# K kept in two rings of key tiles, and filled work spread in groups of six pairs

## The chip, the cores and the metric

The kernel runs on one core of one Trainium2 chip. The metric is the device time of one execution in microseconds (us); lower is better. The core has five engines with queues of their own: TensorE (PE in the profile; its weight loads are PEld), VectorE (DVE), ScalarE (ACT), GpSimd (POOL) and SyncE (SP, which here only issues DMAs).

## The reference

One transformer block on 2048 tokens of width 512, in float32, with modulation vectors made from a condition `c`:

```python
sa, ca, ga, sb, cb, gb = split(silu(c) @ w_mod)        # six vectors of 512
h = layernorm(x) * (1 + ca) + sa
q, k, v = heads(h @ wqkv)                              # 32 heads of 16
p = softmax(q @ k.T / 4)                               # full, 2048 x 2048 for each head
x = x + ga * ((p @ v) @ wo)
h = layernorm(x) * (1 + cb) + sb
x = x + gb * ((silu(h @ w_gate) * (h @ w_up)) @ w_down)   # inner width 1792
```

## The kernel before

Matrix operands are held as a high and a low part, and each product is the sum of three terms (high by high, high by low, low by high). For attention the three terms are stacked in the contraction: a head's 16 rows become 48 (`KR`), plus 2 rows for the shift of the softmax. So a head uses half of TensorE's 128 rows, and two matmuls on different row halves run side by side.

**Units.** The queries are cut into 4 chunks of 512, the heads into 8 groups of 4. A unit `u` (of 32) is one chunk and one head group. A unit has 16 steps, one for each tile of 128 keys; a step has 4 pairs, one for each head. There are 2048 pairs in all. A pair (`pair_of`) is

- a score matmul (`score`, L506): keys by queries, into a score bank; ScalarE takes its exponential (L508) into a tile `pt`;
- on the other row half a max matmul (`max_one`, L479), 20 steps (80 pairs) ahead: queries by 512 keys, into a max bank; VectorE takes the largest of each row (L481).

When the 64 maxima of a unit are there, `max_rows` reduces them (L486), and `rows` transposes -max with matmuls against `ident` and `minus` (L491 to L493), copies it as two rows (`mr`) and writes them by DMA (L497) into the last 2 contraction rows of that unit's `qop`. Against rows of ones in `kop` they shift the scores, so no exponential overflows. `max_rows` puts five entries into the list `side`; each pair runs one of them.

**Value product.** `pv_step` (L521) multiplies the exponentials with V in halves of a step, 4 matmuls on 32 columns each; `pvs` issues several halves in a burst after each group of pairs. V has a column of ones, so the sums of the exponentials (the denominators) come out with the product.

**Unit end.** `close_unit` copies the result to `o`, sends its denominators by DMA into `dn` (`out_a`, L532), loads K and q of unit `u + 3`, and sets later work by step with `at(step, f)`: `out_b` takes the reciprocal on VectorE (L536) and stores it, `out_r` loads it spread over 128 partitions (`rb`), `out_c` multiplies on POOL (L548) and stores the attention rows in DRAM. After the last unit of a chunk the rows are read back (`load_o`) and split (`split_o`).

**K.** Three whole buffers `kop[u % 3]` of 2048 keys; a unit's load (`load_k`, L404) is two DMAs of 768 KB, one issued by SP, one by POOL.

**Fills.** The rest of a chunk (output projection, norm, gate and up, down) fills TensorE's time under the pairs of later units. A job of `accumulate` yields one fill at a time, two matmuls on the two row halves (L718). Two schedules call `pair_of`:

- `plain(steps)`: windows of 3 pairs and then 1 or 2 halves of the value product; 4 max banks, 3 score banks;
- `filled(places, work)`: after pair `r` come `places[r]` fills, and after the group a burst of up to 6 halves; 3 max banks, 2 score banks (4 and 5), the other two hold the job's sums. A gate and up job has 24 fills in two groups `TWO` of 8 pairs, a down job 12 fills in two groups `ONE` of 4 pairs:

```python
TWO = (0, 3, 2, 2, 2, 2, 1, 0)
ONE = (0, 3, 3, 0)
```

In order: projections; a lead of 20 steps with maxima alone; then for chunk `ci` a plain lead to step `STARTS[ci]`, 4 groups of the output projection, 12 plain steps (norm, transposes), for the last of them `REST` more, then the jobs. A plain window (`WIN` steps) stands before a chunk's last down jobs. `posts` (run by `hook` after a group) holds VectorE's and POOL's part of a job. The last 7 jobs (`KEEP`) and the whole of chunk 3 come after the pairs, with full-height matmuls (L727).

`wo` (the output weights, in two `wgu` buffers), `wgu` and `wd` are split once during the first chunk and kept in DRAM (`wo_dr`, `gu_dr`, `wd_dr`).

Of the kernel before, what the change touches and what calls it, by code (L numbers as in the profile page):

```python
# [19 lines left out]
P = 128  # L20
# [26 lines left out]
REST = 24  # L47
NORM = 9
STARTS = (147, 275, 403)
TWO = (0, 3, 2, 2, 2, 2, 1, 0)  # L50
ONE = (0, 3, 3, 0)
ALONE = {TWO: ((0, 4, 0, 4, 0, 4, 0, 0), (4, 5, 0, 1, 5, 0, 4, 1)), ONE: ((0, 6, 0, 0), (4, 5, 4, 0))}

# [48 lines left out]
def block_kernel(ctx, tc, x, wqkv, wo, w_gate, w_up, w_down, c, w_mod, out):  # L102
# [21 lines left out]
    ident = const.tile([P, P], F32, name="ident")  # L124
    minus = const.tile([P, P], F32, name="minus")
    eps_t = const.tile([P, 1], F32, name="eps_t")
# [88 lines left out]
    kop = [vp.tile([P, 2, S], F32R, name="kop0"), None, None]  # L215
# [47 lines left out]
    nc.gpsimd.tensor_scalar_mul(minus, ident, -1.0)  # L263
# [137 lines left out]
    def load_parts(dst, src, g, c0, c1, second=nc.sync):  # L401
        heads = src[g * 64:(g + 1) * 64, :, c0:c1].rearrange("(s b d) r c -> b (d r) s c", s=2, b=2)
# [3 lines left out]
    def load_k0(ci):  # L406
        load_parts(kop[0][:, :, ci * CW:(ci + 1) * CW], kd, 0, ci * CW, (ci + 1) * CW)
# [3 lines left out]
    for b in range(2):  # L411
        nc.sync.dma_start(kop[0][64 * b + KR:64 * b + KR + 2].bitcast(F32).rearrange("p s (a c) -> p (s a) c", c=CW),
                          ones[:, None, :].to_broadcast([2, 2 * NC, CW]))
    kq = [(w, m) for m in range(NK) for w in (1, 0)]
    for ci in range(NC - 1):
# [12 lines left out]
        for i, _ in enumerate(sm.jobs(jobs)):  # L428
            if ci == 0 and i == 5:
                half_prep(1, ev)  # L430
                take(weights_, 2)
                sm.add("w", 5, weights_)
            if ci == 0 and i == 24:
                sm.add("p", 5, prep(pa, xt[1], hT[1], 0, 1))
            if i == 40:
                load_k0(ci)
            if i == 44 and ci + 2 < NC:
                load_x(ci + 2)
# [11 lines left out]
    kop[1] = pb.tile([P, 2, S], F32R, name="kop1", bufs=1)  # L450
    pf = None
    qop, mx, pts, pv, o_, due, res = {}, {}, {}, {}, {}, {}, {}
    posts = []
    n = 16 * NU
    last = NC - 1

    def ones_rows(k):
        for b in range(2):
            rows = slice(64 * b + KR, 64 * b + KR + 2)
            nc.sync.dma_start(kop[k][rows].bitcast(F32), kop[0][rows].bitcast(F32))  # L460

    def load_k(u):
        load_parts(kop[u % 3], kd, u % NG, 0, S, nc.gpsimd if u > 2 else nc.sync)

    def load_q(u):
        ci, g = divmod(u, NG)
        qop[u] = pb.tile([P, 2, CW], F32R, name="qop", tag="qop", bufs=3)
        load_parts(qop[u], qd, g, ci * CW, (ci + 1) * CW, nc.gpsimd if u > 2 else nc.sync)

    def max_one(r):  # L470

        u, t = divmod(r // 4, 16)
        b, e = 1 - r % 4 // 2, r % 2
        s, qt, kc = t // 8, t // 2 % 4, t % 2 * 2 + e
# [4 lines left out]
        nc.tensor.matmul(pm, qop[u][rows, s, qt * P:(qt + 1) * P], kop[u % 3][rows, s, kc * CW:(kc + 1) * CW],  # L479
# [3 lines left out]
    def max_rows(u):  # L483

        m = pb.tile([P, 16], F32, name="m", tag="m")
        nc.vector.tensor_reduce(m, mx.pop(u).rearrange("p b s t f -> p (b s t) f"), op=ALU.max, axis=AX.X)  # L486
        nm = pb.tile([P, 16], F32R, name="nm", tag="nm")

        def rows():
            pr = bank("pr")[0:16, 0:2 * P]  # L490
            nc.tensor.matmul(pr[:, 0:P], nm.bitcast(F32), ident, start=True, stop=True)  # L491
            nc.tensor.matmul(pr[:, P:2 * P], m, minus, start=True, stop=False)
            nc.tensor.matmul(pr[:, P:2 * P], nm.bitcast(F32), minus, start=False, stop=True)  # L493
            mr = pb.tile([16, 2, P], F32R, name="mr", tag="mr", bufs=1)
            nc.scalar.copy(mr, pr.rearrange("p (r q) -> p r q", r=2))
            for r in range(2):
                nc.sync.dma_start(qop[u][KR + r:KR + r + 65:64].bitcast(F32), mr[:, r, :].bitcast(F32))  # L497
        side.extend([lambda: None, lambda: None, lambda: nc.scalar.mul(nm, m, -1.0), lambda: None, rows])

    def score(i, h):  # L500
# [5 lines left out]
        nc.tensor.matmul(sp, kop[u % 3][rows, h // 2, kt * P:(kt + 1) * P], qop[u][rows, h // 2, :],  # L506
# [120 lines left out]
    class Chunk:  # L627
# [15 lines left out]
        def load_wo(self, places=None):  # L643
            self.wo = places or [as_wo(tile_gu()) for _ in range(NK // 2)]
            for k, w in enumerate(self.wo):
                (nc.sync if self.ci == 0 else nc.gpsimd).dma_start(w.bitcast(F32), wo_dr[k])

        def load_gu(self, f):
            if f < NF and f not in self.loaded:
                self.loaded.add(f)  # L650
                self.w[f] = self.places[f % len(self.places)] if self.places else tile_gu()
                nc.sync.dma_start(self.w[f].bitcast(F32), gu_dr[f])
# [99 lines left out]
    def out_pair(ch, t0, outs, halves):  # L752
        return accumulate(outs, lambda e, a, k: ch.oT[a][:, k, (t0 + e) * P:(t0 + e + 1) * P],
                          lambda b, k: ch.wo[k // 2][:, b, k % 2, :], NK,
                          lambda: posts.append(lambda: add_o(ch, t0, outs, True)), halves)

    def out_terms(ch, t, pt, ks):
        for k in ks:
            for a, b in ((0, 0), (0, 1), (1, 0)):
                nc.tensor.matmul(pt, ch.oT[a][:, k, t * P:(t + 1) * P], ch.wo[k // 2][:, b, k % 2, :],  # L760
                                 start=(k == 0 and a == b == 0), stop=(k == NK - 1 and a == 1))

    def gate_up(ch, f, outs, halves):
# [20 lines left out]
        return accumulate(outs, lambda e, a, k: w[:, 2 * e + a, k, :], lambda b, k: ch.hT[b][:, k, :], NK, after,  # L784
# [25 lines left out]
    def begin(ci):  # L810
        x2 = pf.tile([P, 4, D], F32, name="x2", tag="x2", bufs=1)
        act = [pf.tile([P, NK, CW], F32R, name=f"act{a}", tag=f"act{a}", bufs=1) for a in range(2)]
        hT = [pf.tile([P, NK, CW], F32R, name=f"act{a}", tag=f"act{a}", bufs=1) for a in range(2)]
        chunks[ci] = ch = Chunk(ci, x2, act, hT)
# [12 lines left out]

    late = sm.jobs([proj_T(last, w, m) for w, m in kq[:1] + kq[2:]] + [proj_T(last - 1, w, m) for w, m in kq[6:]] +
                   [proj_T(last, *kq[1])] + [proj_v(4 * ci + t) for ci in (last - 1, last) for t in range(4)])
    ones_rows(1)  # L830
    load_q(0)
    take(late, 22)
    load_k0(last)
    take(late, 26)

    def close_unit(u, i):
# [11 lines left out]
        if u % NG == NG - 1:  # L848
            if u // NG:
                at(i + 1, lambda: begin(u // NG))  # L850
                at(i + 1, lambda: chunks[u // NG].load_wo())
            at(i + 7, lambda: chunks[u // NG].load_o(nc.gpsimd))
            at(i + 9, lambda: chunks[u // NG].split_o())

    at(3, lambda: begin(0))
# [4 lines left out]
    def after(i):  # L860
# [6 lines left out]
        if i == -2:  # L867
# [4 lines left out]
            kop[2] = pf.tile([P, 2, S], F32R, name="kop2")  # L872
            ones_rows(2)
            load_k(2)
# [4 lines left out]
    for i in range(-LEAD, -1):  # L879
        if i == -LEAD + 3:  # L880
            load_k(1)
# [5 lines left out]
        while side:  # L887
            side.pop(0)()

# [15 lines left out]
    def pvs(most, by_halves):  # L905
# [4 lines left out]
        while most and halves and 4 * halves[0][0] + 8 <= done:  # L910
# [16 lines left out]
    def plain(steps, tails=()):  # L927
# [4 lines left out]
        for w in range(4 * steps // WIN):  # L932
            for _ in range(WIN):
                pair_of()
            if w >= 4 * steps // WIN - len(tails):
                tails[w - 4 * steps // WIN](four())
# [3 lines left out]
    def filled(places, work):  # L940
# [14 lines left out]
    def two_of(u):  # L955
        return [kop[u % 3][:, e, :].rearrange("p (k c) -> p k c", k=NK) for e in range(2)]

    def begin_last():
# [100 lines left out]
```

## Time and profile before

| | us |
|---|---|
| median of 3 runs | 1921.11 |
| the runs | 1927.79, 1919.36, 1921.11 |
| span of the profiled execution, first to last instruction | 1926.2 |
| TensorE busy in it | 1876.4 (97%) |
| VectorE busy | 1541.1 (80%) |
| ScalarE busy | 1250.8 (65%) |
| POOL busy | 418.6 (22%) |

The profile gives the span of its own execution; what that execution took as a whole is not told beside it. A busy share on TensorE is no measure of its rate, since matmuls overlap: the two of a pair run side by side, and so do the two of a fill. The views used below are the page itself; stages (busy time of each engine between two times, with the granted TensorE clock, the share of the DMA engines and GB/s at the end of each row); instructions in order of time (start, duration, engine, line, operation, shapes, and in brackets the idle time before it and what ended it); and waits (who waited for whom: total, times, longest).

### The profile page before, as it was taken

The page shows a single profiled execution, that of the slowest core. Times are in us where ns is not written, and L with a number is a line of the kernel's source. Part 1 is how long each engine was busy: PE and PEld are TensorE (multiplying, and loading weights), DVE is VectorE, ACT ScalarE, POOL GpSimd, SP SyncE. Part 2 cuts the span into 40 slices and gives each one's busy share as a digit, 9 for nine tenths or more (in the row PEclk, how much of TensorE's full clock was granted, in tenths as well). Part 3 has the DMA queues.
Part 4 walks back from the last instruction along what each step waited for, and adds up shares of the span by engine and source line. Part 5 has one row for each costly group of instructions (what it writes and reads, how often), then busy time and mean ns, then how long its engine had stood idle before and what let it go on. Part 6 is the DMA issues. An engine that isn't in the chain of part 4 may idle for free.

```text
span 1926.2 us, 40835 instructions
## 1 busy us (share of the span) xinstructions
PE 1876.4 (97%) x16996; PEld 1149.1 (60%) x16996; DVE 1541.1 (80%) x2558; ACT 1250.8 (65%) x2330; POOL 418.6 (22%) x504
## 2 busy tenths in 40 slices
PE   7999999999999999999899999999899999999999
PEld 5766444444455666666455666666455466667787
DVE  5458998999989888888789888888799988841643
ACT  4222887788877766667677766776677876674211
POOL 3000344555322211111123111111133011021200
PEclk9999999999999999999899999999899999999999
DMA  8764766667753534553544544453543354253642
GB/s 299 265 219 121 187 161 161 190 180 185 192 90 74 141 99 113 148 133 84 130 81 90 121 114 131 116 141 76 135 81 76 54 141 119 73 177 122 237 194 109
DMA packets 78340, 267.60 MB, mean 139 GB/s; under 512 B 17364, under 2 KB 22484, under 8 KB 57476
## 3 DMA queue, kind: packets, MB, share of 16 engines
q1 hardware_dynamic: 58188, 173.81, 31.7%
q0 software_dynamic: 19280, 90.39, 19.5%
q8 instruction: 133, 2.18, 0.5%
q10 hardware_dynamic: 688, 0.80, 0.1%
q14 instruction: 51, 0.42, 0.1%
HBM read 201.85 MB, written 62.13 MB: 137 GB/s over the span
## 4 chain that ended last, share of the span: by engine, by line
PE 89%; DMA 5%; DVE 3%; ACT 2%; SPq 0%; issue 0%; ACTq 0%; DVEq 0%
PE bank L521 25%; PE bank L506 20%; PE bank L718 18%; PE bank L479 9%; PE bank L727 7%; PE bank L209 6%; DMA dn<-o 4%; DVE mx L481 1%; PE bank L760 1%; PE bank L491 1%; DVE stt L743 1%; PE bank L162 0%; PE bank L703 0%; DMA wm_ab<-in_w_mod 0%; PE bank L493 0%
## 5 line engine op out<-in xcount | busy, mean ns | idle before, releaser
L481 DVE TENSOR_REDUCE mx<-bank 128x1 f32<-128x512 f32 x2048 | 1285.6, 683 | 146.9 <-PE bank L479 97.7
L479 PE MATMUL bank<-kop,qop 48*128 48x512 f32 x2048 | 766.2, 439 | 26.4 <-DVE mx L481 25.0
L506 PE MATMUL bank<-qop,kop 50*128 50x512 f32 x2048 | 757.4, 433 | 3.8 <-DMA qop<-mr 0.9
L506 PEld LDWEIGHTS bank<-qop,kop 50*128 50x128 f32 x2048 | 349.0, 187 | 315.6 <-issue 54.5
L479 PEld LDWEIGHTS bank<-kop,qop 48*128 48x128 f32 x2048 | 347.3, 187 | 59.2 <-DVE mx L481 42.4
L718 PE MATMUL bank<-act,wgu 64*128 64x512 f32 x1872 | 295.4, 393 | 0.0
L718 PEld LDWEIGHTS bank<-act,wgu 64*128 64x128 f32 x1872 | 184.3, 187 | 32.6 <-issue 0.2
L548 POOL TENSOR_TENSOR on<-o,rb 128x512 f32<-128x512 f32 x31 | 39.8, 1283 | 527.4 <-DMA rb<-d_dr 379.4
L718 PE MATMUL bank<-wd,mid 64*128 64x512 f32 x912 | 130.5, 392 | 0.0
L779 POOL CAST mid<-m 128x512 fp32r<-128x512 f32 x40 | 24.5, 612 | 345.4 <-PE bank L479 164.8
L209 PE MATMUL bank<-hT,wqs 128*128 128x512 f32 x384 | 95.8, 400 | 2.3 <-ACT hT L328 1.0
L718 PEld LDWEIGHTS bank<-wd,mid 64*128 64x128 f32 x912 | 88.7, 186 | 15.3 <-issue 0.7
L209 PEld LDWEIGHTS bank<-hT,wqs 128*128 128x128 f32 x384 | 70.4, 188 | 24.3 <-issue 6.1
L775 DVE SCALAR_TENSOR_TENSOR q<-th,bank 128x512 f32<-128x512 f32 x56 | 38.1, 681 | 56.8 <-ACT th L771 56.8
L771 ACT ACTIVATE th<-bank 128x512 f32<-128x512 f32 x56 | 33.3, 594 | 58.5 <-PE bank L727 58.4
L791 DVE TENSOR_TENSOR x<-bank,x 128x512 f32<-128x512 f32 x84 | 53.9, 685 | 19.6 <-PE bank L718 19.6
L369 DVE TENSOR_TENSOR prt<-bank,prt 128x512 fp32r<-128x512 f32 x32 | 22.0, 689 | 45.5 <-ACT prt L367 45.5
L367 ACT CAST prt<-bank 128x512 fp32r<-128x512 f32 x32 | 18.8, 586 | 58.6 <-PE bank L209 46.8
L777 DVE TENSOR_TENSOR m<-bank,q 128x512 f32<-128x512 f32 x56 | 38.7, 692 | 21.1 <-PE bank L727 19.1
L727 PE MATMUL bank<-wd,mid 128*128 128x512 f32 x216 | 52.3, 395 | 0.5 <-DVE mid L780 0.3
L780 POOL TENSOR_TENSOR mid<-m,mid 128x512 fp32r<-128x512 f32 x40 | 51.5, 1288 | 3.3
L718 PE MATMUL bank<-wgu,act 64*128 64x512 f32 x288 | 47.9, 395 | 0.1
(6282 smaller groups left out, 5196.9 us busy)
## 6 DMA issues: line engine op xcount, KB each, us to landing
wgu<-gu_dr SPq DMA_DIRECT2D x48, 1024.0 KB
wd<-wd_dr SPq DMA_DIRECT2D x28, 1024.0 KB
kop<-kd SPq DMA_DIRECT2D x33, 768.0 KB
kop<-kd POOLq DMA_DIRECT2D x29, 768.0 KB, 8.4
gu_dr<-wgu POOLq DMA_DIRECT2D x14, 1024.0 KB, 4.9
kd<-prt SPq DMA_DIRECT2D x16, 512.0 KB
qd<-prt SPq DMA_DIRECT2D x16, 512.0 KB
kop<-gu_dr SPq DMA_DIRECT2D x8, 1024.0 KB
```

The source lines that it names most:

```text
L209: nc.tensor.matmul(pt, lhs(a, k), rhs(b, k), start=(n == 0), stop=(n == 3 * nk - 1))
L479: nc.tensor.matmul(pm, qop[u][rows, s, qt * P:(qt + 1) * P], kop[u % 3][rows, s, kc * CW:(kc + 1) * CW], start=True, stop=True)
L481: nc.vector.tensor_reduce(mx[u][:, b, s, qt, kc:kc + 1], pm, op=ALU.max, axis=AX.X)
L506: nc.tensor.matmul(sp, kop[u % 3][rows, h // 2, kt * P:(kt + 1) * P], qop[u][rows, h // 2, :], start=True, stop=True)
L521: nc.tensor.matmul(pv[u][32 * h:32 * h + 32, cols], v_flat[:, e0:e0 + 32], p_[h][:, cols], start=(kt == 0 and half == 0), stop=(kt == 15), ...
L548: mul.tensor_mul(on, o, rb)
L718: nc.tensor.matmul(outs[e], lhs(e, a, k)[rows], rhs(b, k)[rows], start=(ph == 0 and j == 0), stop=(ph == 1 and j == z))
L727: nc.tensor.matmul(outs[e], lhs(e, a, k), rhs(b, k), start=(j == 0), stop=(j == z))
L775: nc.vector.scalar_tensor_tensor(q, th, 1.0, outs[0], op0=ALU.add, op1=ALU.mult)
L777: nc.vector.tensor_mul(m32, outs[1], q)
L780: (nc.gpsimd if slow else nc.vector).tensor_sub(mid[:, 1, :], m32, mid[:, 0, :].bitcast(F32))
L791: nc.vector.tensor_add(ch.x2[:, t, :], outs[e], ch.x2[:, t, :])
```

## The change

- K lives in two rings of four tiles of 512 keys, `kop[u % 2][c]`. Each tile is loaded for unit `u + 2` when unit `u`'s scores have passed it (`at(16 * u + 4 * c + 3, ...)`), by two DMAs of 192 KB, both on SP, as are q's. The maxima of a unit go through the key tiles in order.
- The memory of the third K buffer holds a second pair of activation tiles, so the attention rows of a chunk are read back and split two units at a time.
- Part of the jobs is spread thinner: groups `SIX` of 6 pairs and 6 fills. Gate and up jobs up to a limit (`THICK`, 8, 8 and 5 for the three chunks) take four of these in place of two `TWO`, down jobs two in place of two `ONE` (now called `FOUR`). The plain leads of chunks 1 and 2 come to length 0, the windows before the last down jobs go, `REST` is halved, `STARTS` are 3 steps earlier. After a group the burst is 3 halves where it ends in the middle of a step.
- The rows of -max come from two products instead of three, four pairs after the copy that they need, and at the end of a group, ahead of the burst.
- At a unit's end the reciprocal comes 5 steps after closing instead of 3, the spread load 6 instead of 4, the product 8 instead of 5.
- The output weights of the next chunk are loaded before a chunk's last down jobs. For the last chunk they go into the K ring as its tiles come free, and two gate and up tiles are loaded right after the pairs.
- `minus` is made on VectorE.

```diff
-REST = 24
-STARTS = (147, 275, 403)
+STARTS = (144, 272, 400)
+REST = 12
+THICK = (8, 8, 5)
 TWO = (0, 3, 2, 2, 2, 2, 1, 0)
-ONE = (0, 3, 3, 0)
+SIX = (0, 2, 2, 1, 1, 0)
+FOUR = (0, 3, 3, 0)
+LATE = (0, 0, 0, 3, 3, 0)
...
-    nc.gpsimd.tensor_scalar_mul(minus, ident, -1.0)
+    nc.vector.tensor_scalar_mul(minus, ident, -1.0)
...
+    def load_k(u, ci):
+        load_parts(kop[u % 2][ci], kd, u % NG, ci)
...
+    kop[1] = [pb.tile([P, 2, CW], F32R, name=f"kop1{c}", bufs=1) for c in range(NC)]
+    nms = [pb.tile([P, 2, 16], F32R, name=f"nm{e}", bufs=1) for e in range(2)]
...
     def max_one(r):
-        b, e = 1 - r % 4 // 2, r % 2
-        s, qt, kc = t // 8, t // 2 % 4, t % 2 * 2 + e
+        b, s = 1 - r % 4 // 2, r % 2
+        kc, qt = divmod(t, 4)
...
     def max_rows(u):
-        m = pb.tile([P, 16], F32, name="m", tag="m")
-        nc.vector.tensor_reduce(m, mx.pop(u).rearrange("p b s t f -> p (b s t) f"), op=ALU.max, axis=AX.X)
+        m = pb.tile([P, 2, 16], F32, name="m", tag="m")
+        for_rows = mx.pop(u).rearrange("p b s t f -> p (b s t) f")[:, None].to_broadcast([P, 2, 16, NC])
+        nc.vector.tensor_reduce(m, for_rows, op=ALU.max, axis=AX.X)
+        nm = nms[u % 2]
         def rows():
-            nc.tensor.matmul(pr[:, 0:P], nm.bitcast(F32), ident, start=True, stop=True)
-            nc.tensor.matmul(pr[:, P:2 * P], m, minus, start=True, stop=False)
-            nc.tensor.matmul(pr[:, P:2 * P], nm.bitcast(F32), minus, start=False, stop=True)
+            nc.tensor.matmul(pr, m.rearrange("p r h -> p (r h)"), minus, start=True, stop=False)
+            nc.tensor.matmul(pr, nm.rearrange("p r h -> p (r h)").bitcast(F32), ident, start=False, stop=True)
...
-        side.extend([lambda: None, lambda: None, lambda: nc.scalar.mul(nm, m, -1.0), lambda: None, rows])
+        wait = [lambda: None] * 3
+        side.extend(wait + [lambda: nc.scalar.copy(nm[:, 1, :], m[:, 0, :])] + wait + [lambda: tails.append(rows)])
...
+        def load_wo_part(self, k):
+            nc.gpsimd.dma_start(kop[0][k].bitcast(F32), wo_dr[k // 2][:, :, k % 2, :])
+            self.wo = lambda b, k: kop[0][k][:, b, :]
...
     def begin(ci):
+        oT, hT = [[pf.tile([P, NK, CW], F32R, name=f"act{ci % 2}{a}", tag=f"act{ci % 2}{a}", bufs=1) for a in range(2)]
+                  for _ in range(2)]
...
+    for c, t in enumerate(kop[1]):
+        for b in range(2):
+            own = slice(64 * b + KR, 64 * b + KR + 2)
+            nc.sync.dma_start(t[own].bitcast(F32), kop[0][c][own].bitcast(F32))
     load_q(0)
...
         if u + 3 < NU:
-            load_k(u + 3)
             load_q(u + 3)
-        at(i + 3, lambda: res.__setitem__(u, out_b(u, nc.sync, *res[u])))
-        at(i + 4, lambda: res.__setitem__(u, out_r(u, nc.sync, *res[u])))
-        at(i + 5, lambda: out_c(u, nc.gpsimd, nc.gpsimd, *res.pop(u)))
+        at(i + 5, lambda: res.__setitem__(u, out_b(u, nc.sync, *res[u])))
+        at(i + 6, lambda: res.__setitem__(u, out_r(u, nc.sync, *res[u])))
+        at(i + 8, lambda: out_c(u, nc.gpsimd, nc.gpsimd, *res.pop(u)))
+        if u % 2 and u < NU - 2:
+            at(i + 10, lambda: chunks[u // NG].load_o(nc.gpsimd, (u % NG // 2,)))
+            at(i + 12, lambda: chunks[u // NG].split_o((u % NG // 2,)))
+    for u in range(NU - 2):
+        for c in range(NC):
+            at(16 * u + 4 * c + 3, lambda u=u, c=c: load_k(u + 2, c))
...
     def filled(places, work):
         for r in range(len(places)):
             pair_of()
             take(work, places[r])
-            if r % 4 == 3:
-                end_steps()
+            end_steps()
         hook()
-        pvs(6, False)
+        flush()
+        pvs(3 if done % 4 else 6, False)
+
+    def window(ch, job, args):
+        thick = (args[0] if job is gate_up else 2 * args[0]) >= THICK[ch.ci]
+        if job is down:
+            if args == (NF // FG - 1, 0):
+                return (FOUR, FOUR) if thick else (LATE, SIX)
+            return (FOUR if thick else SIX,) * 2
+        return (TWO,) * 2 if thick else (SIX,) * 4
...
             if args == (NF // FG - 1, 0):
-                plain(WIN)
+                chunks[ci + 1].load_wo()
+            places = window(ch, job, args)
             work = job(ch, *args, outs, True)
-            for _ in range(2):
-                filled(TWO if job is gate_up else ONE, work)
+            for group in places:
+                filled(group, work)
+        if ci < last - 1:
+            rows_of(chunks[ci + 1])
...
+    ch.places = [[kop[r][2 * k + e] for e in range(2)] for r in (1, 0) for k in range(2)]
+    for f in range(2):
+        ch.load_gu(f)
```

More of the change, by code (lines that the diff above doesn't have):

```diff
@@ L214, in block_kernel @@
     vp = ctx.enter_context(tc.tile_pool(name="vp", bufs=1))
-    kop = [vp.tile([P, 2, S], F32R, name="kop0"), None, None]
+    kop = [[vp.tile([P, 2, CW], F32R, name=f"kop0{c}") for c in range(NC)], None]
     VW = NT * H * (DH + 1)
@@ L478, in max_one @@
         pm = four("pm")
-        nc.tensor.matmul(pm, qop[u][rows, s, qt * P:(qt + 1) * P], kop[u % 3][rows, s, kc * CW:(kc + 1) * CW],
+        nc.tensor.matmul(pm, qop[u][rows, s, qt * P:(qt + 1) * P], kop[u % 2][kc][rows, s, :],
                          start=True, stop=True)
@@ L505, in score @@
         sp = bank("st_")
-        nc.tensor.matmul(sp, kop[u % 3][rows, h // 2, kt * P:(kt + 1) * P], qop[u][rows, h // 2, :],
+        nc.tensor.matmul(sp, kop[u % 2][kt // 4][rows, h // 2, kt % 4 * P:(kt % 4 + 1) * P], qop[u][rows, h // 2, :],
                          start=True, stop=True)
@@ L810, in begin, with rows_of @@
     def begin(ci):
[L811 to L814, printed above, removed]
+        oT, hT = [[pf.tile([P, NK, CW], F32R, name=f"act{ci % 2}{a}", tag=f"act{ci % 2}{a}", bufs=1) for a in range(2)]
+                  for _ in range(2)]
+        chunks[ci] = Chunk(ci, None, oT, hT)
+    def rows_of(ch):
+        ch.x2 = pf.tile([P, 4, D], F32, name="x2", tag="x2", bufs=1)
         ch.load_x2(nc.gpsimd)
@@ L880, in block_kernel @@
         if i == -LEAD + 3:
-            load_k(1)
+            for c in range(NC):
+                load_k(1, c)
             load_q(1)
@@ L909, in pvs @@
             most, owed = most + owed, 0
-        while most and halves and 4 * halves[0][0] + 8 <= done:
+        while most and halves and 4 * halves[0][0] + (6 if done % 4 == 2 and not by_halves else 8) <= done:
             i, half = halves.pop(0)
@@ L925, in end_steps, with plain @@
             ended += 1
-    def plain(steps, tails=()):
+    def plain(steps, ends=()):
         nonlocal four, bank
@@ L934, in plain @@
                 pair_of()
-            if w >= 4 * steps // WIN - len(tails):
-                tails[w - 4 * steps // WIN](four())
+            if w >= 4 * steps // WIN - len(ends):
+                ends[w - 4 * steps // WIN](four())
+            flush()
             pvs((HALVES[(w - 2) % 4] if done > 8 else 0) + (w == 4 * steps // WIN - 1), True)
@@ L1023, in block_kernel @@
     take(rest, 48)
-    ch.places = [tile_gu() for _ in range(2)]
-    for u in (NU - 3, NU - 2):
-        ch.places += [kop[u % 3][:, k, :].rearrange("p (a k c) -> p a k c", a=4, k=NK) for k in range(2)]
-    ch.ahead = 4
-    for f in range(ch.ahead):
+    ch.places += [tile_gu() for _ in range(2)]
+    for f in range(2, ch.ahead):
         ch.load_gu(f)
```

98 lines of the change are left out of this document (44 added, 54 removed).

## The prediction

> **What bounds the kernel now.** I read the page's head first, then the stages cut at group boundaries, then the order of time inside one group, and last the waits of the stages that lose.
>
> ```profile
> span 1926.2 us, 40835 instructions
> PE 1876.4 (97%) x16996; PEld 1149.1 (60%) x16996; DVE 1541.1 (80%) x2558; ACT 1250.8 (65%) x2330; POOL 418.6 (22%) x504
> ```
> ```profile
> core 0: us, PE busy (x) PEld busy (x) DVE busy (x) ACT busy (x) POOL busy (x), PEclk, DMA share, GB/s
> 188.00:566.00 378.00, 370.00 (x3568) 170.95 (x3568) 357.60 (x606) 313.20 (x616) 171.85 (x176) 0.96 0.67 170
> 628.00:908.00 280.00, 280.00 (x2912) 185.09 (x2912) 240.83 (x382) 194.91 (x350) 42.17 (x49) 1.00 0.48 121
> 931.00:995.00 64.00, 55.05 (x510) 24.74 (x508) 51.26 (x87) 45.02 (x88) 16.58 (x23) 0.87 0.58 130
> 1360.00:1425.00 65.00, 56.75 (x510) 25.59 (x509) 51.31 (x87) 44.99 (x88) 16.54 (x23) 0.87 0.57 128
> 1487.00:1546.00 59.00, 58.58 (x590) 27.41 (x590) 58.12 (x99) 51.16 (x102) 6.79 (x8) 1.00 0.32 66
> 1762.00:1926.00 164.00, 159.79 (x720) 128.49 (x712) 69.31 (x117) 27.03 (x45) 10.77 (x14) 1.00 0.46 177
> ```
>
> A pair is one score and one max matmul. 1487 to 1546 is plain work of 96 pairs: 0.615 us a pair, and VectorE is busy for 58.1 of 59 us, so plain work sits on VectorE with TensorE just under it. 628 to 908 is filled work of chunk 0: VectorE has 39 us to spare and TensorE none. The three leads (588, 84 and 84 pairs) are plain too, but take 378, 64 and 65 us where 0.615 gives 361.6, 51.7 and 51.7: 16.4, 12.3 and 13.3 us are lost there.
>
> Inside one filled group:
>
> ```profile
> 709.53 0.42 PE L506 MATMUL bank<-qop,kop 50*128 50x512 f32 x1
> ...
> 711.75 0.50 PE L506 MATMUL bank<-qop,kop 50*128 50x512 f32 x1
> ...
> 712.09 0.40 PE L506 MATMUL bank<-qop,kop 50*128 50x512 f32 x1
> ...
> 713.02 0.41 PE L506 MATMUL bank<-qop,kop 50*128 50x512 f32 x1
> ...
> 713.96 0.40 PE L506 MATMUL bank<-qop,kop 50*128 50x512 f32 x1
> ...
> 715.30 0.49 PE L506 MATMUL bank<-qop,kop 50*128 50x512 f32 x1
> ```
>
> 711.75 to 715.30 is a group of 4 pairs and 6 fills (places 0, 3, 3, 0): the first two pairs are 0.34 apart, and three fills with the next pair take 0.93, so a place for a pair or a fill is 0.233 us. The last pair with two halves of the value product takes 1.34; 709.53 to 711.75 is the same with four halves, 2.22. A half is thus 0.44 us, and each burst of them costs 0.46 beside.
>
> A score bank is given back late:
>
> ```profile
> 708.37 0.39 PE L506 MATMUL bank<-qop,kop 50*128 50x512 f32 x1
> 708.80 0.60 ACT L508 ACTIVATE pt__7769<-bank 128x512 f32<-128x512 f32 x1
> 709.45 0.18 PEld L506 LDWEIGHTS bank<-qop,kop 50*128 50x128 f32 x1 [0.19 <-ACT pt__7769 L508]
> ```
> ```profile
> 712.29 0.60 ACT L508 ACTIVATE pt__7814<-bank 128x512 f32<-128x512 f32 x1 [1.22 <-PE bank L479]
> ```
> ```profile
> 712.32 1.89 DVE L481 TENSOR_REDUCE mx<-bank 128x1 f32<-128x512 f32 x3 [0.18 <-PE bank L479]
> ```
>
> With two score banks, the pair of 709.53 waited for the exponential of 708.37: 0.43 to its start, 0.60 for it, 0.13 to the next matmul, 1.16 in all; just after a burst the first part is 0.54 (711.75 to 712.29), 1.27 in all. Five places are 1.165, so the old groups just fit. Three maxima take 1.89, 0.63 each.
>
> **The change part by part.**
>
> *Groups.* Counted from the code, the filled work now takes 128 groups of 6 pairs and 6 fills. They replace 42 groups of 8, 44 groups of 4, and 252 plain pairs: the leads of chunks 1 and 2, 12 pairs of the first lead, 24 before the last down jobs, 48 of the rest.
> What goes: a group of 4 is 3.55 above, and I take 3.6 with unit ends; the 28 groups of 8 and 24 of 4 in 628 to 908 then give (280 − 86.4) / 28 = 6.91. So 42 × 6.91 + 44 × 3.6 = 448.6; the plain pairs are 64 + 65 + 84 × 0.615 = 180.7. Together 629.3 us.
> What comes: places 0, 2, 2, 1, 1, 0 with banks 4 and 5. Pair 1 at 0.34; pair 2 would be at 0.34 + 0.70 = 1.04, but its bank comes at 1.27; pair 3 at 1.97; pair 4 at 2.44 (its bank at 2.43); pair 5 would be at 2.90, its bank comes at 1.97 + 1.16 = 3.13; then 0.46 + 3 × 0.44 = 1.78. Sum 4.91, and 4.95 with the shares of -max rows and unit ends; 128 × 4.95 = 633.6.
> Net +4.3 us: four places instead of five between two users of a bank cost 0.46 a group, and eat what 39 bursts fewer would bring. Bounds: 4.50 if the bank waits do not bind (58 us less), and 5.3 if all six exponentials queue at 0.60 ahead of the burst (6 × 0.60 + 1.78; 45 us more). I take 4.95, nearest to the rows. VectorE needs 6 × 0.63 + 0.7 for the additions, 4.5, so it stays hidden by 0.45.
>
> *Later unit end and ring loads.* The losses of the leads are waits for the denominators:
>
> ```profile
> DVE dn L536 <- DMA dn<-o: 9.0, 5, 2.8
> ```
> ```profile
> DVE dn L536 <- DMA dn<-o: 9.5, 1, 9.5
> ...
> PE bank L479 <- DVE mx L481: 8.6, 1, 8.6
> ```
> ```profile
> 962.00:972.00 10.00, 10.00 (x69) 4.28 (x65) 6.85 (x12) 5.09 (x10) 4.16 (x6) 0.58 0.20 59
> ```
> ```profile
> 322.00:332.00 10.00, 8.97 (x57) 3.97 (x59) 7.46 (x13) 4.09 (x8) 0.00 (x0) 0.66 0.48 80
> ```
>
> The first row is of the first lead, the two next of chunk 1's. The reciprocal stands on VectorE ahead of the maxima, so TensorE stops for want of max banks, and then runs at a granted 0.58 to 0.66 for 10 us. Now the reciprocal comes two steps (8 × 0.615 = 4.9 us) later, more than the longest wait of the first lead (2.8), and the 1.5 MB of K no longer go out behind the denominators but in quarters. I count the 16.4 us of the first lead as gone; the two long ones are already in the 629.3, and their cause (x, output weights, K and q at once) is spread out. Bounds: −16.4 and 0.
> The Trainium skill ("TensorE: Matmul & The Clock Gate", Part 1) says that the clock is halved only after an idle window of about 3.4 us. By that, waits up to 2.8 us cost only themselves, 9.0 us, and the forecast below would be 1912. The row of 322 to 332 disagrees: 0.66 after a stop well under that.
> What the later end moves on POOL (scaling at +8, the read-back of attention rows at +10) lies on an engine that is 22% busy. Out jobs start 14 steps after their last unit closes.
> K's loads leave POOL's queue for SP's: eight issues a unit in place of two, each queued behind mr and the denominators. They are asked for nine steps (36 × 0.615 = 22 us) before they are read, against
>
> ```profile
> kop<-kd POOLq DMA_DIRECT2D x29, 768.0 KB, 8.4
> ...
> wgu<-wo_dr POOLq DMA_DIRECT2D x4, 1024.0 KB, 21.1
> ...
> kop<-wo_dr POOLq DMA_DIRECT2D x2, 1024.0 KB, 9.0
> ```
> 8.4 us for four times the bytes: nothing. Bounds 0 and the price of the slower rival below.
>
> *Rows of -max.*
>
> ```profile
> 704.05 0.49 PE L506 MATMUL bank<-qop,kop 50*128 50x512 f32 x1
> ...
> 704.49 0.39 PE L491 MATMUL bank<-ident,nm 128*16 128x128 f32 x2
> ...
> 705.25 0.50 PE L506 MATMUL bank<-qop,kop 50*128 50x512 f32 x1
> ```
> Two pairs are 1.20 apart where 0.34 is usual: 0.86 a unit for six instructions. Four remain, put ahead of a burst, and the copy they wait for is four pairs old: I take 0.5, so 0.36 × 19 units outside the new groups, −7 us (bounds −16 and 0). They are issued at least 8 pairs (4.9 us) before the scores that need them. VectorE's reduction reads twice the elements:
> ```profile
> L486 DVE TENSOR_REDUCE m<-mx 128x16 f32<-128x64 f32 x32 | 6.9, 216 | 0.9
> ```
> at most another 0.22 us a unit, under the slack of the groups; 0.
>
> *Start and end.* The ones rows of the second K take eight issues on SP instead of two ahead of the first q:
>
> ```profile
> 119.33 1.43 SPq L460 DMA_DIRECT2D kop<-kop  x2
> ```
> ```profile
> 131.95 0.59 PE L479 MATMUL bank<-kop,qop 48*128 48x512 f32 x2 [1.15 <-DMA kop<-kd]
> ```
> Six more at 0.72 are 4.3 us; the wait of 1.15 for the last part of K goes, since maxima now run by key tile. I take +2 (0 to +4). The minus matrix moves from POOL to an idle VectorE: 0. At the end TensorE is busy for 159.8 of 164 us, so earlier loads and the new places are worth 0 (−4 to +1).
>
> Sum: +4.3 − 16.4 − 7 + 2 = −17.1 us, off a span of 1926.2. What lies around the span is not shown; it is 5.1 us above the median of the runs, 1921.1, from which I take the same 17 us: 1904.
>
> **The rivals.**
> *Bank waits do not bind.* For it: ScalarE is at 65%. Against it: the 0.19 at 709.45. A group then takes 4.50, and 58 us more go: 1846.
> *Only the waits count, not the clock* (the skill's rule above): 1912.
> *The unit-end wait stays.* If the denominators land more than 5 steps after they are asked for, VectorE stops as now. For it: all of K, q, weights and rows are now on SP's queue. Against it: less is in flight at that moment. Half of the 42 us lost in the leads returns: 1925, no change.
> *Output weights late, the side of slower.* Their load now starts when the last gate job of a chunk ends, behind a cast and a subtraction on POOL:
>
> ```profile
> L779 POOL CAST mid<-m 128x512 fp32r<-128x512 f32 x40 | 24.5, 612 | 345.4 <-PE bank L479 164.8
> ...
> L780 POOL TENSOR_TENSOR mid<-m,mid 128x512 fp32r<-128x512 f32 x40 | 51.5, 1288 | 3.3
> ```
> With the issues that is 3 us, and four groups of 4 (14.4 us) are left until the out job reads them. At 21.1 us (issued with 3 MB of others) they are 9.7 us late, and ten microseconds at 0.58 add 4.2; twice, 28 us: 1932. It decides from a landing above 11.4 us; at 9.0, as at the end of the kernel, nothing is lost.
>
> **How the numbers follow.** Forecast 0.52; clock rule 0.06; no bank waits 0.10; unit-end wait stays 0.16; weights late 0.16. The forecast's own range is 1888 to 1920 (groups of 4.85 to 5.05, rows and start at their bounds). The range, 1865 to 1930, leaves out the case of 1846 and about half of the slower one. Half a per cent, about 9.6 us, is what a measurement of this kernel can tell from no change. Faster: nine tenths of the forecast, the free banks, half of the clock case, 0.60; same 0.24; slower 0.16.
>
> **What would show it.** Groups of six: 4.9 us from first pair to first pair, with weight loads of L506 held by ScalarE at the third and sixth pair; at 4.5 or below my bank step is wrong. The wait of the denominators' reciprocal
> ```profile
>   DMA dn<-o: 34.3, 8
> ```
> falls to under 12 us (some 7 of it are in the tail, with nothing behind it), and the granted clock of the first lead goes to 1.00; if not, the unit-end step is wrong. Pairs around the rows of -max lie 0.5 apart from the rest, not 0.86. A TensorE gap in front of the out jobs, with a wait for the output weights, speaks for the slower rival.

## The result, and the profile after

The changed kernel takes 1975.4 us (median of 4 runs, 1971.9 to 1980.3) against 1922.2 for the kernel before (4 runs): a ratio of 1.0273, 95% interval 1.0251 to 1.0296. It is slower by 2.7%, where 1904 was forecast. The profiled execution took 1974.3 us, with a span of 1972.1, 45.9 more than before. Its page:

```profile
span 1972.1 us, 41216 instructions
PE 1909.4 (97%) x16932; PEld 1154.3 (59%) x16932; DVE 1535.0 (78%) x2561; ACT 1249.9 (63%) x2330; POOL 386.2 (20%) x447
```

VectorE and ScalarE do the same work as before in more time, and TensorE is again 97% busy: the page alone does not tell where 46 us went. The stages do, cut at the start of the first pair of each group:

| us of span | before | after | difference | forecast |
|---|---|---|---|---|
| up to the first score | 187.7 | 187.8 | +0.1 | +2 |
| first lead (before: without its last 12 pairs) | 370.6 | 379.2 | +8.6 | −16.4 |
| filled groups, other leads, rest | 1101.5 | 1124.9 | +23.4 | +4.3 |
| norms and transposes | 101.4 | 101.9 | +0.5 | 0 |
| after the last pair | 164.9 | 178.2 | +13.3 | 0 |
| rows of -max (inside the stages above) | | | | −7 |
| sum | | | +45.9 | −17.1 |

What TensorE waited for in the changed kernel (who waited for whom: total, times, longest):

```profile
PE bank L507 <- DMA qop<-mr: 13.4, 5, 4.7
PE bank L522 <- ACT o L526: 12.0, 16, 0.9
PE bank L772 <- ACT act L679: 9.9, 1, 9.9
```

None of the three stood in the trace before at such a size. They are scores waiting for the rows of -max, the value product waiting for ScalarE's copy of a finished unit, and the last output projection waiting for the last attention rows. TensorE's own wait for max banks, which VectorE frees, was 25.0 us in 13 before and is 1.5 in 5 now. The wait of the reciprocal, which the change was to shorten, is down from 34.3 us in 8 to

```profile
  DMA dn<-o: 10.6, 1
```

and that one is in the tail. So the unit end did what was forecast, and yet the first lead did not get shorter. Its stage, and the ten microseconds behind four of the five waits for the rows (the fifth, of 3.04 us, ended at 317.25; the clock was 0.71 over the next ten):

```profile
188.00:567.00 379.00, 364.28 (x3476) 170.25 (x3474) 350.07 (x594) 304.20 (x603) 161.54 (x158) 0.95 0.51 165
270.00:280.00 10.00, 10.00 (x60) 4.04 (x64) 5.95 (x10) 5.85 (x11) 4.19 (x6) 0.50 0.94 337
399.30:409.30 10.00, 9.99 (x104) 4.59 (x104) 8.58 (x15) 8.07 (x16) 7.16 (x9) 1.00 0.49 135
480.00:490.00 10.00, 10.00 (x72) 4.26 (x74) 5.99 (x10) 6.04 (x12) 8.14 (x9) 0.66 0.27 84
523.00:533.00 10.00, 9.89 (x68) 4.20 (x68) 6.35 (x10) 5.91 (x11) 0.00 (x0) 0.57 0.67 245
```

The granted clock is 0.95 over the lead, against 0.96 before: new stops took the place of the old ones. The first, in order of time (a product and a DMA issue of POOL, the DMA issue of the rows on SyncE, and the score that waits for them):

```profile
252.68 1.28 POOL L549 TENSOR_TENSOR on<-o,rb 128x512 f32<-128x512 f32 x1 [32.35 <-DMA rb<-d_dr]
...
261.88 0.58 POOL L588 DMA_DIRECT2D wd_dr<-wd  x1 [0.30 <-POOL wd L585]
262.53 1.82 SPq L496 DMA_DIRECT2D qop<-mr  x2
269.79 0.76 PE L507 MATMUL bank<-qop,kop 50*128 50x512 f32 x1 [4.68 <-DMA qop<-mr]
```

The score was ready at 269.79 − 4.68 = 265.11, only 2.6 us after the rows (two DMAs of 8 KB) were issued, and it started 7.3 us after that issue; the last DMA packet of the rows ended 6.1 us after it. The 1 MB store of split weights went out 0.65 us ahead of them. The nine units behind the first show the same: in the five that TensorE waited for, a 1 MB store left POOL between 1.31 us ahead of the rows and 0.60 behind, and their last packet ended 3.4 to 6.1 us after the issue; in the other four no store left that close, and it ended after 2.0 us. Before, the same two steps of POOL:

```profile
250.59 1.29 POOL L548 TENSOR_TENSOR on<-o,rb 128x512 f32<-128x512 f32 x1 [16.97 <-ACT pt__2191 L508]
...
266.51 0.58 POOL L587 DMA_DIRECT2D wd_dr<-wd  x1 [0.30 <-POOL wd L584]
```

The third piece of weights that POOL splits in each unit is asked for at step 8, as the unit end's product now is. So it stands right behind that product, which waits for its denominators, and its store comes 9.2 us after the product began. Before, the product came at step 5, the piece of that step (with two stores to `gu_dr`) stood between the two, and the store left 15.9 us after the product began, 5.0 us after the rows (then issued at 261.50).

A plain group of six in a thin stage (three halves at the end; PE, then the weight loads of the same window):

```profile
1140.66 0.49 PE L507 MATMUL bank<-qop,kop 50*128 50x512 f32 x1
1141.00 0.39 PE L507 MATMUL bank<-qop,kop 50*128 50x512 f32 x1
...
1141.85 0.49 PE L507 MATMUL bank<-qop,kop 50*128 50x512 f32 x1
...
1143.73 0.49 PE L507 MATMUL bank<-qop,kop 50*128 50x512 f32 x1
...
1145.59 0.49 PE L507 MATMUL bank<-qop,kop 50*128 50x512 f32 x1
```
```profile
1141.84 0.18 PEld L507 LDWEIGHTS bank<-qop,kop 50*128 50x128 f32 x1 [0.42 <-ACT pt__12858 L509]
...
1143.73 0.18 PEld L507 LDWEIGHTS bank<-qop,kop 50*128 50x128 f32 x1 [0.41 <-ACT pt__12881 L509]
```

It takes 4.93 us, with weight loads held by ScalarE at the third and at the sixth pair. A group whose burst runs over a unit's end takes 5.9 to 6.0 (ScalarE's copy, then the product that needs its bank):

```profile
1109.74 0.58 ACT L526 COPY o<-bank 128x512 f32<-128x512 f32 x1 [0.43 <-PE bank L522]
```
```profile
1110.38 0.40 PE L522 MATMUL bank<-pt__12450,v_flat 128*32 128x256 f32 x1 [0.70 <-ACT o L526]
```

The tail: its start as a stage; ScalarE's queue, which sends and fetches the last denominators, and SyncE's loads of the two tiles (four of 512 KB: three go out ahead of the denominators, from 1794.96 on, and one behind; 2 MB for other jobs left just before); and the two transfers on the chain that ended last:

```profile
1794.00:1830.00 36.00, 26.07 (x129) 19.95 (x127) 5.54 (x10) 3.90 (x7) 0.00 (x0) 0.83 0.48 168
```
```profile
1795.44 10.85 SPq L660 DMA_DIRECT2D kop<-gu_dr  x3
1797.07 1.11 ACTq L533 DMA_DIRECT2D dn<-o  x1
1806.21 0.35 ACTq L538 DMA_DIRECT2D d_dr<-dn  x1
```
```profile
1797.07 8.83 DMA dn<-o
1809.99 8.05 DMA rb<-d_dr
```

Before, the same two steps of ScalarE's queue lay 3.3 us apart, not 9.1:

```profile
1765.36 1.12 ACTq L532 DMA_DIRECT2D dn<-o  x1
1768.67 0.35 ACTq L537 DMA_DIRECT2D d_dr<-dn  x1
```

### The profile page after: what moved, and what is told of

It reads as the page before. It is cut to its first block, busy times and chain, and to the rows that moved or that the text cites. A ratio compares the mean times of both kernels' runs of the same rounds, so it can differ in the third digit from the quotient of the medians.

```text
span 1972.1 us, 41216 instructions
## 1 busy us (share of the span) xinstructions
PE 1909.4 (97%) x16932; PEld 1154.3 (59%) x16932; DVE 1535.0 (78%) x2561; ACT 1249.9 (63%) x2330; POOL 386.2 (20%) x447
## 4 chain that ended last, share of the span: by engine, by line
PE 89%; DVE 4%; DMA 3%; ACT 3%; issue 1%; SPq 0%; POOL 0%; ACTq 0%; DVEq 0%; POOLq 0%
PE bank L522 24%; PE bank L507 24%; PE bank L730 18%; PE bank L478 8%; PE bank L739 7%; PE bank L213 6%; DVE mx L480 3%; DMA qop<-mr 1%; ACT o L526 1%; PE bank L491 1%; DMA dn<-o 0%; DMA rb<-d_dr 0%; PE bank L166 0%; PE bank L715 0%; PE bank L283 0%
## 5 line engine op out<-in xcount | busy, mean ns | idle before, releaser
L507 PE MATMUL bank<-qop,kop 50*128 50x512 f32 x2048 | 786.7, 441 | 16.2 <-DMA qop<-mr 13.4
L478 PE MATMUL bank<-kop,qop 48*128 48x512 f32 x2048 | 795.3, 446 | 3.2 <-DVE mx L480 1.5
L730 PE MATMUL bank<-act,wgu 64*128 64x512 f32 x1872 | 319.6, 393 | 0.4 <-DVE m L789 0.3
L730 PEld LDWEIGHTS bank<-act,wgu 64*128 64x128 f32 x1872 | 195.6, 186 | 27.7 <-DVE m L789 3.9
L730 PE MATMUL bank<-wd,mid 64*128 64x512 f32 x912 | 151.9, 395 | 0.9 <-POOL mid L792 0.9
L730 PEld LDWEIGHTS bank<-wd,mid 64*128 64x128 f32 x912 | 93.6, 186 | 15.4 <-DVE m L789 2.5
L739 PE MATMUL bank<-act,kop 128*128 128x512 f32 x240 | 57.2, 396 | 0.0
```

Of the source, the lines that this page charges most:

```text
L507: nc.tensor.matmul(sp, kop[u % 2][kt // 4][rows, h // 2, kt % 4 * P:(kt % 4 + 1) * P], qop[u][rows, h // 2, :], start=True, stop=True)
L730: nc.tensor.matmul(outs[e], lhs(e, a, k)[rows], rhs(b, k)[rows], start=(ph == 0 and j == 0), stop=(ph == 1 and j == z))
L739: nc.tensor.matmul(outs[e], lhs(e, a, k), rhs(b, k), start=(j == 0), stop=(j == z))
```

## The experiments

After the result the theory had three parts: the rows of -max come too late (first lead), the early gate and up loads hold back the last denominators (tail), and the groups of six cost more than what they replace. The rival for the rows was that lateness alone does it, against lateness together with the moved store. The kernel before took 1922.9, 1922.6 and 1921.2 us beside these runs.

**Rows of -max two pairs after the copy, inside the group, as before** (e1)

```diff
-        side.extend(wait + [lambda: nc.scalar.copy(nm[:, 1, :], m[:, 0, :])] + wait + [lambda: tails.append(rows)])
+        side.extend([lambda: None, lambda: None, lambda: nc.scalar.copy(nm[:, 1, :], m[:, 0, :]), lambda: None, rows])
```

> Changed kernel with one edit: the rows of -max are made at the fifth pair after the maxima, as before the change, not at the end of a group. In the changed kernel TensorE waits 13.4 us in the first lead for the DMA of these rows, and then runs at a low clock; the lead takes 379 us where 351 was forecast. Theory 'asked too late': the rows now leave with 3.8 to 7.3 us to the first score in place of 4.7 to 6.8; asked as before, the wait goes under 1 us, the lead falls to about 357 us, and with 0.36 us a unit paid back for rows in mid-group the time is about 1960 us. Theory 'behind a store': the rows land late because a 1 MB store of split weights now leaves POOL within a microsecond of them (261.9 against 262.5 us); asked one microsecond earlier they still meet it, the wait stays above 5 us, and the time is 1970 us or more.

Measured: 1947.4 us, ratio 1.0132 (1.0111 to 1.0154), 28 us less than the changed kernel, more than any theory had given. The first lead takes 354.3 us, and in the waits no row for `mr` is left above the two others:

```profile
PE bank L521 <- ACT o L525: 12.0, 16, 0.9
PE bank L771 <- ACT act L678: 9.5, 1, 9.5
```

So the rows cost the lead 25 us in these two profiles. In e1's the clock was 0.50 from 192.70 to 206.35 us, at the lead's start and behind no wait for rows, and 1.00 from 210 on; e9 below has the same lead at full clock, 349.2 us. Against that the rows cost 30 us: 13.4 of waits and 16.6 behind them, near the 19 us that a granted 0.95 leaves out of 379.2. This run does not yet part the two theories: asked earlier, the rows leave 1.4 us or more ahead of the store, not beside it as the second theory expected, and land in 2.0 to 2.3 us.

**The weights' third piece ahead of the unit end's product on POOL, rows left late** (e2)

```diff
-        if 0 <= i < UG and i % 16 in (3, 5, 8):
+        if 0 <= i < UG and i % 16 in (3, 5, 7):
```

> Changed kernel with one edit: the third piece of weight splitting in each unit of the first chunk is issued after step 7 of the unit in place of step 8, so on POOL's queue it stands ahead of the unit end's product (now at step 8), not behind it. Theory 'behind a store': the 1 MB store leaves some 25 us earlier, meets no rows of -max, TensorE's wait for them goes from 13.4 us to under 2, the first lead from 379 to about 355 us, the time to about 1950 us. Theory 'asked too late': nothing changes, 1975 us.

Measured: 1955.3 us, 1.0166 (1.0149 to 1.0183), lead 358.3. Moving a store, with no edit to the rows, takes away two thirds of their wait (all but 2 us was expected to go):

```profile
PE bank L507 <- DMA qop<-mr: 4.3, 3, 3.5
```

The longest that is left, 3.5 us, is of rows that meet another store, of a gate and up tile, issued 0.53 us after them.

**The late rows alone, in the kernel before** (e6: `rows` with two products, the three waits and the flush ahead of a burst)

> The kernel before with the new rows of -max alone (two products, one copied four pairs earlier, made at the end of a group, some 3 us later than before). The unit end, K and the groups are as before, so the store of weights leaves at 266 us, after the rows of that unit. Theory 'behind a store': lateness alone costs nothing; TensorE's wait for the rows stays under 2 us, and 0.36 us a unit are saved: 1910 to 1918 us. Theory 'asked too late': the first lead stops for the rows, waits of 5 us or more in total, 1930 us or more.

Measured: 1917.3 us, 0.9976 (0.9962 to 0.9989).

```profile
PE bank L511 <- DMA qop<-mr: 4.1, 4, 1.9
```

The same lateness without the moved store costs 4.1 us of waiting, between the two theories (under 2, or 5 and more), and is still a small gain. Three of its four waits are of rows with a gate and up store 1.4 to 2.5 us ahead of them, which landed in 4.1 to 5.1 us; where no store left in the 3 us ahead, they landed in 2.0 to 2.6 and cost 0.3 us at most. e2 and e6 together settle it: late rows leave no reserve, and the store next to them makes it 13.4 us.

**The first two gate and up tiles of the tail loaded where they were** (e3)

```diff
-    for f in range(2):
-        ch.load_gu(f)
...
-    for f in range(2, ch.ahead):
+    for f in range(ch.ahead):
```

> Changed kernel with one edit: the first two gate and up tiles of the last chunk are loaded where they were before the change, not ahead of the last unit's end. Theory 'loads in front': the last denominators took 8.8 us to land and the spread load 8.1 because 2 MB go out ahead of them, so TensorE stops for 9.9 us at 1816 us and runs slower after; without them they land in about 3 and 5 us, the stop goes, and the time is 1962 us. Rival: the stop comes from the new places of the attention rows; then 1975 us.

Measured: 1961.8 us, 1.0199 (1.0182 to 1.0215); the tail takes 168.2 us in place of 178.2, and its wait is

```profile
PE bank L772 <- ACT act L679: 1.7, 1, 1.7
```

Ten of the 13.3 us lost at the end are these loads. The denominators, which reached VectorE 8.9 us after they were sent, do so in 4.2; in the kernel before it was 3.0, with the 2 MB for other jobs sent 2.5 us earlier.

**Fills in threes between pairs, so that a bank has more time to come back** (e4)

```diff
-SIX = (0, 2, 2, 1, 1, 0)
+SIX = (0, 3, 0, 3, 0, 0)
```

> Changed kernel with one edit: the fills of a group of six stand at places 0, 3, 0, 3, 0, 0 in place of 0, 2, 2, 1, 1, 0. Theory 'score banks': a group takes 4.93 us because the third and the sixth pair wait for a score bank; with three fills between the second and the third pair and between the fourth and the fifth only the sixth still waits (its exponential queues behind the one before it), a group takes 4.70, 128 of them 29 us less: 1946 us. Rival 'max banks or VectorE': two pairs side by side ask for max banks faster than VectorE frees them, and the group stays at 4.9 or grows: 1975 us or more.

Measured: 1957.2 us, 1.0197 (1.0161 to 1.0232). The plain group went from 4.93 to 4.73 us, near what was expected of it; but all 128 together went from 648.0 to 636.2 only, 11.8 of the 21.0 us between the two profiled spans (the medians are 18 apart). Most of the rest is a first lead of 369.5 us, which the edit does not touch, so that part is no gain of the places. What the groups take over 128 plain ones rose from 16.5 to 31.6 us; a part of it is a job's first groups, whose early fills now wait for VectorE:

```profile
PE bank L730 <- DVE m L789: 3.0, 14, 0.6
```

**The later unit end alone, in the kernel before** (e5)

```diff
-        at(i + 3, lambda: res.__setitem__(u, out_b(u, nc.sync, *res[u])))
-        at(i + 4, lambda: res.__setitem__(u, out_r(u, nc.sync, *res[u])))
-        at(i + 5, lambda: out_c(u, nc.gpsimd, nc.gpsimd, *res.pop(u)))
+        at(i + 5, lambda: res.__setitem__(u, out_b(u, nc.sync, *res[u])))
+        at(i + 6, lambda: res.__setitem__(u, out_r(u, nc.sync, *res[u])))
+        at(i + 8, lambda: out_c(u, nc.gpsimd, nc.gpsimd, *res.pop(u)))
...
-            at(i + 7, lambda: chunks[u // NG].load_o(nc.gpsimd))
-            at(i + 9, lambda: chunks[u // NG].split_o())
+            at(i + 10, lambda: chunks[u // NG].load_o(nc.gpsimd))
+            at(i + 12, lambda: chunks[u // NG].split_o())
```

> The kernel before with the later unit end alone: reciprocal, spread load and product at 5, 6 and 8 steps after closing in place of 3, 4 and 5, the read-back and split of a chunk's attention rows 3 steps later. Theory: the unit-end step of the forecast was right, and only covered by other losses: the first lead falls from 378 to about 362 us, the leads of chunks 1 and 2 lose at least 5 of their 12 to 13 us each, and the time is 1885 to 1897 us. Rival: the wait moves with the reciprocal, or the product, now later on POOL's queue, pushes a store of weights onto the rows of -max: 1915 to 1925 us.

Measured: 1901.0 us, 0.9892 (0.9878 to 0.9907), a gain, but above the 1897 expected at most. The first lead takes 360.8 us, near the prediction's 361.6. The leads of chunks 1 and 2 come to 60.5 and 59.7 us only, not to 51.7: VectorE still waits there for the denominators, 6.3 and 5.9 us. Whole K buffers and output weights are in flight then; that these are the cause was not tried. VectorE's idle time ahead of the reciprocal in all (7.7 us of it are in the tail):

```profile
  DMA dn<-o: 21.2, 4
```

**Early rows and late tail loads together** (e9: the edits of e1 and e3), **and with the places of e4** (e8)

> Changed kernel with the early rows and the late tail loads, groups of six as in the change: the plain reference for the run with the old groups (1882.6 us). If the two losses add, 1975 - 28 - 13.6 = 1934 us, and the groups alone cost 50 us; if the old groups had also removed other waits, this run is under 1925 us and the groups cost less.

> Changed kernel with early rows, late tail loads and the places 0, 3, 0, 3, 0, 0 together. If the three losses stand in different places, they add: 28 + 13.6 + 18 us off 1975 gives 1916 us, no slower than the kernel before. If part of them is the same time twice, 1925 us or more.

Measured: e9 1937.8 us, 1.0087 (1.0067 to 1.0107); e8 1924.1, 1.0007 (0.9998 to 1.0017). In e9 nothing is lost in the first lead any more, 349.2 us for its 576 pairs at full clock:

```profile
188.00:537.00 349.00, 348.59 (x3478) 163.25 (x3478) 348.52 (x594) 303.68 (x603) 161.57 (x158) 1.00 0.57 179
```

The places are worth 14 us, and by the groups' sums 16 (651.3 to 635.1); e8 lies 8 us above what adding the single runs promised, which fits e4's gain having been in part the lead's. What e9 still loses must lie in the groups.

**The old groups with all the rest of the change** (e7: the edits of e9, and)

```diff
-STARTS = (144, 272, 400)
-REST = 12
-THICK = (8, 8, 5)
+STARTS = (147, 275, 403)
+REST = 24
+THICK = (0, 0, 0)
...
+    filled((0,) * 4, iter(()))
```

All jobs then run in `TWO` and `FOUR`, the leads come back with 96 pairs each, and a group of four pairs without fills closes the pairs.

> Changed kernel with the early rows and the late tail loads of the two runs so far, and with the old groups: groups of 8 for all gate and up jobs, of 4 for all down jobs, plain leads of 24 steps, 24 steps of rest. The two edits alone should give about 1934 us. Theory 'the groups cost': 128 groups of six take 651 us in the trace; 42 groups of 8 (6.9), 44 of 4 (3.6) and 252 plain pairs at 0.615 take 603: 48 us less, 1886 us. Rival 'the leads lose it again' (unit ends wait in plain leads as before the change): 1910 us or more.

Measured: 1882.6 us, 0.9795 (0.9781 to 0.9810), 55 us less than e9. The first lead and chunk 1's:

```profile
188.00:544.00 356.00, 355.43 (x3545) 166.21 (x3548) 355.56 (x606) 310.32 (x615) 161.68 (x158) 1.00 0.55 176
902.00:960.00 58.00, 57.88 (x584) 27.08 (x582) 57.80 (x99) 50.70 (x102) 5.88 (x8) 1.00 0.29 87
```

Both at full clock with VectorE busy throughout: 0.61 us a pair, and no stop. The losses of chunk 1's and 2's leads are gone without any group of six.

**A burst that stops at a unit's end** (e10: e9, and)

```diff
-                if by_halves:
+                if by_halves or done % 4:
                     break
```

> The run before this one with one more edit: where a group of six ends in the middle of a step, its burst of the value product stops at a unit's end, and the next unit's first half waits for the next burst. In the changed kernel a burst runs on into the next unit 16 times, TensorE then stands 12.1 us in all for ScalarE's copy of the result, and such a group takes 5.9 to 6.0 us where others take 4.93. By the code 5 of the 16 go. Theory 'burst across a unit's end': the wait falls to about 8.5 us, five groups lose 1 us each, 5 us less than the run before. Rival 'unit ends cost by other work': same time, same groups of 6 us.

Measured: 1933.7 us, 1.0058 (1.0044 to 1.0073), 4 us below e9, where 5 was expected, with intervals that overlap a little; the wait itself fell from 12.0 us in 16 to

```profile
PE bank L521 <- ACT o L525: 8.3, 11, 0.9
```

**The old groups with the rows at the end of the group in which e7's stand** (e11: e7 with `lambda: tails.append(rows)` for `rows`), **and the weights' third piece earlier** (e12: e11 with the edit of e2)

> The run with the old groups (1882.6 us), with the rows of -max issued at the end of the group in which the early rows would stand (asked at the fifth pair, then behind the group, ahead of the burst). Theory: as the rows then need no place between two pairs, 0.36 us a unit are saved, some 8 us in all without a new wait: 1874 us. Rival: the rows come up to 7 pairs later in groups of eight and meet the store of weights in the first lead; waits over 3 us, 1882 us or more.

> The run before this one with the third piece of weight splitting issued one step earlier, ahead of the unit end's product. If rows and store still meet, this takes the rest of the wait away: 1 to 4 us less than the run before. If they no longer meet, the same time within 2 us.

Measured: e11 1878.4 us, 0.9773 (0.9758 to 0.9787); e12 1879.5, 0.9776 (0.9761 to 0.9791). No wait for `mr` is left in e11, so there was none for e12 to take away. e11 is the fastest version, though e12 is within the spread of its runs: 43 us below the kernel before and 97 below the changed one.

```profile
span 1875.6 us, 41233 instructions
PE 1846.3 (98%) x16932; PEld 1148.7 (61%) x16932; DVE 1535.7 (82%) x2561; ACT 1240.4 (66%) x2330; POOL 386.8 (21%) x447
```

## Why the prediction was wrong, and where it was right

Of the miss of 63 us in span, 19.1 lie in the groups, 25.0 in the first lead, 13.3 at the end, and 7 is the gain of the rows that never showed; the start gave back 1.9, and 0.5 is in the norms.

*Rows of -max: the step that failed first.* "They are issued at least 8 pairs (4.9 us) before the scores that need them" was counted in places of the code. In the trace the first of the waiting scores is due 2.6 us after the issue. The bound of the term went from −16 to 0, so it had no side on which the rows are late at all. Nor did the sentence on the later product on POOL, "an engine that is 22% busy", follow what is queued behind it: the weights' store, which now leaves beside the rows. The runs showed in its place: beside a store the rows take 3.4 to 6.1 us to land, TensorE waits 13.4 us for them and runs at the lower clock behind, and the lead grew by 8.6 us where 16.4 were to go. The size of the rows' own work was right: a group with them in it takes 5.41 us against 4.93, 0.48 more, where 0.5 was taken; in e9, with the rows back among the pairs, 20 groups with rows or a unit's end in them are dearer by 17.8 us, 0.89 each. Worth of the move where nothing is late: 4.1 us (e7 to e11; 2.7 when each is set against the kernel before beside it), not 7.

*End: the second.* "Earlier loads and the new places are worth 0 (−4 to +1)" looked at TensorE's busy share in the tail and not at what the loads travel beside. The last denominators and their spread load are on the path; without the tiles, of which 1.5 MB go out in front of the denominators, the stop goes from 9.9 to 1.7 us, and the tail is 10.0 us shorter (e3).

*Groups: the mechanism right, the size too small, and the comparison wrong.* The bank step was right, and its sum close in part by luck: 4.93 us, with ScalarE holding the third and sixth pair, where 4.91 was worked out. The third pair came at 1.19 us in place of 1.27 and the sixth at 3.07 in place of 3.13, but the rest took 1.86 in place of 1.78. The rival of free banks (4.50) is out. But 4.95 was taken as the mean, and the mean is 5.06: 648.0 − 633.6 = 14.4 us. Of the 16.5 us above the plain group, 5.7 are 12 groups with the rows and 8.1 are 8 groups whose burst of three halves runs over a unit's end, where the product waits for ScalarE's copy (of its 12.0 us in all, the rest is in other groups). The prediction took a share for unit ends but not this wait; before, weight loads had waited for that copy for 5.3 us in 17. Another 5.6 us are groups of the old kinds that got slower (2.8 in the jobs, 2.8 in the output projection); the work that went measures 630.3 us in the trace before, 1.0 above the 629.3 of the sum.

The larger fault is in what the 633.6 us were set against. The 629.3 us "removed" held the 25.6 us that the leads of chunks 1 and 2 lost to late denominators, and so the groups were credited with taking these away. e7 shows that the later unit end and the spread loads do it with the leads in place: 58.4 and 58.9 us for 96 pairs. Quiet old work, by e7's rows, is 42 × 6.89 + 44 × 3.64 + 252 × 0.61 = 603 us. Against it the forecast's own groups were 30 us of loss; measured (651.3 in e9) they are 48, and with the other groups and the tail e9 is 55 us behind e7 by span. The groups alone turn a change worth −40 us (e7) into one that costs 17 (e9); late rows and early tail loads make it 53.

Two slips in the sums changed nothing: 6 × 0.60 + 1.78 is 5.38, not 5.3, and 86 groups and 84 plain windows have 42 bursts more than 128 groups, not 39. The bounds named for the forecast's own range, simply added, give 1880 to 1926, wider than its 1888 to 1920.

*Right:* the unit end. The first lead of e5 came to 360.8 us (361.6 forecast), and the waits for the denominators fell as said. Its sign, a first lead at clock 1.00, failed in the changed kernel because of the rows (0.95), and holds without them (1.00 in e9). TensorE waits for no load of the K rings, the start moved by 0.1, and the output weights of the slower rival were not late: no stop stands in front of the out jobs. So the chance given to slower stood on a step that did not fail, and the steps that did fail had been given little or no slower side.

*What stays open:* e1 and e2 gave 28 and 20 us, more together than the 30 us that the lead lost; each cures most of the same wait, so they need not add, but no run had both. Why e1's profiled lead began with 13.65 us at half clock (the 5 us between it and e9's) is not known; its other three runs were 5.8 to 7.5 us shorter. And of the 15 us by which e4's groups rose over plain ones, waits on VectorE are 3.0.

## What to carry to other kernels

When work is spread thinner, work out how soon each buffer must come back in the new order: here four places of 0.233 us do not cover a bank's 1.16 us, and every group pays. Cost a change against the old code with its own stalls taken out; a stall that another part of the change removes is not this part's gain. A small transfer on the path is judged by what leaves the core around it, on all queues, and an edit that moves one queue's order moves what stands behind it.

## What the hardware showed that was not expected

- The rows of a unit (two DMAs of 8 KB) ended (by their last DMA packet) 2.0 us after their issue in the changed kernel's first lead when no weight store left close to them, and up to 6.1 us beside one of 1 MB; 8 KB of denominators took 8.8 us where 3.5 MB of loads had been sent in the 3 us ahead of them, and 4.2 (e3) where it was 2 MB, against at most 3.3 us from sending to storing them in the tail before.
- The granted clock after a stop does not go by the stop's length alone: over the next ten microseconds it was 0.57 after 1.47 us, 0.66 after 1.95, 1.00 after 2.28, 0.71 after 3.04 and 0.50 after 4.68. The trace's clock records tell more: the clock is 1.00 or 0.50, and in this lead it changes at 268.39, 282.04, 316.18, 323.00, 480.02, 486.84, 524.39 and 534.63 us, all whole multiples of 3.413 us apart. Cut at these steps, the piece before each drop had 3.28, 1.97, 1.95 and 1.47 us of TensorE's idle time in it; the stop of 2.28 us lies across a cut, 1.07 and 1.22 us on its sides, and nothing dropped. No threshold follows: in the kernel before, 1.15 us was enough once (at 325.29 us) and 1.28 once was not (at 1380). The rule of the Trainium skill cited in the prediction ("TensorE: Matmul & The Clock Gate", Part 1, an idle window of about 3.4 us) agrees with these rows in the length of the piece, but not in that the whole of it must be idle: 1.47 us of 3.41 was enough.
